# A gated linear attention and an MLP planned as one instruction list: first scores in other banks, denser filler products, finer pieces, a longer search for the order

## The chip, the cores and the metric

The kernel runs on one core of a Trainium2 chip. The metric is device time in microseconds (us) of one execution. The engines are named as in the profile: PE is TensorE (PEld its weight loads), DVE is VectorE, ACT is ScalarE, POOL is GpSimd, SP is the engine that issues most DMAs. "L795" is line 795 of the kernel before.

## What is computed

The first half is a gated linear recurrence over 768 steps for 4 x 8 heads of width 48; its output, rearranged to 3072 rows of 384, goes through a two-layer MLP with `h - tanh(h)` between the layers.

```python
for t in range(S):
    state = alpha[:, :, t, :, None] * state + np.einsum('bhd,bhe->bhde', k[:, :, t], v[:, :, t])
    y[:, :, t] = np.einsum('bhd,bhde->bhe', q[:, :, t], state)
...
x = np.ascontiguousarray(attn_out.transpose(0, 2, 1, 3)).reshape(B * S, H * D)
h = x @ w_in            # 384 -> 2048
g = h - np.tanh(h)
return (g @ w_out).astype(np.float32)
```

q, k, v and alpha are float32. The weights arrive as 8-byte words and are rounded to float32 on the chip.

## The kernel before

**Units.** The work is cut into 12 units of 256 time steps, all 8 heads of one batch entry each; a unit has two chunks of 128 steps, written `u.0` and `u.1`. For every unit there is an attention part (function `gla`) and an MLP part (`moe`) of 8 steps, written `u:0` to `u:7`.

**Attention part.** alpha, k and q come in by DMA. For unit 0, and for k and q of unit 1, they are turned by products with the identity (`turn`, L663; parts a and b are the even and the odd time steps) into PSUM. For all later ones ACT moves a strip of 16 columns (`widen`, two copies, L633) and DVE transposes 32x32 blocks (`flip`, four instructions, L639). Then DVE scans alpha from behind (`U`, L711), takes the ends (two small operations, L719 and L720) and scans from the front (`W`, L730); k is multiplied with U (`kU`) and q with W (`qW`) (L679 for the turned units). In unit 0 each scan is done in two halves, one for each chunk; in later units it is one instruction over both. After that, for each chunk: `scores` (PE, L795 or L805), `masked` (DVE, L819 or L822), `back`, `natural` and `update` (the state's increment), and `y` (PE, L850 to L860 in unit 0), then a copy into xT (`x`, ACT).

**MLP part.** Step `u:s` has `first` (PE, L1080, 12 products), four element-wise operations on ACT and DVE, and `second` (PE, L1125 in units 0 and 1, L1146 with the combined weights of `combine` after that). Weight pieces `in0` to `in7` and `out0` to `out7` are fetched by SP (L43), read by ACT (`read`, L86 and L87) and finished by DVE (L89 and L90), just ahead of unit 0's steps.

**PSUM.** [...] `ps_sc` holds one tile of two banks (`two_banks()`, name `sc`), `ps_h` two banks (tag `h`), `ps_o` four banks (tags `o0` to `o3`). In unit 0, alpha's turned parts lie in `o0` and `o1`, k's in the two `h` banks, and q's two parts in `sc`. `scores 0.0` then takes `sc` too, so it has to wait until every read of q's turned parts is over; `scores 0.1` takes the two `h` banks. Unit 1's turned q takes `sc` again.

**The order.** No engine's order is written by hand. Every piece of work is a task with an engine, an estimated duration, the tasks it depends on, and a latency to its dependents (0.3 us if nothing else is given). `Planner.run` (L341) is a list scheduler over these estimates; `Planner.order` (L387) calls it in 8 rounds, from the fourth with random noise (deviation 2 us) on the priorities, and keeps the plan that ends first. Two tasks of one engine that depend on each other are 0.3 us apart in it. All instructions are then issued in the order of the planned starts, and each engine works through its own list in that order.

**Filler.** Until the first `y` of unit 0, gaps in PE's plan are filled with products of the identity with itself (`spin`, L1208), whose result nobody reads. The number in each gap is the gap divided by an estimated 0.35 us, rounded down:

```python
filled += [(free, -1, do, None)] * int(max(0.0, x[0] - free) / us)
...
plan.filler = "PE", "y 0.0", 0.35, spin
plan.begin.update(SP=0.8, PE=1.5, ACT=3.0, DVE=4.8)
```

A float32 product leaves two matmul records in the profile.

Of the kernel before, what the change touches and what calls it, by code (L numbers as in the profile page):

```python
# [321 lines left out]
class Planner:  # L322
# [2 lines left out]

    ROUNDS, SEED, NOISE = 8, 1, 2.0

    def __init__(self):  # L330
        self.tasks = []
# [55 lines left out]
    def order(self):  # L387
        names = {t[0]: i for i, t in enumerate(self.tasks)}
        assert len(names) == len(self.tasks)
        before, after = ([[] for _ in self.tasks] for _ in range(2))  # L390
        for i, t in enumerate(self.tasks):
            edges = {names[a]: self.tasks[names[a]][6] for a in t[4]}
            if t[7]:
                edges.setdefault(names[t[7]], 0.0 if self.tasks[names[t[7]]][1] == t[1] else 0.25)
            for j, lat in edges.items():
                before[i].append((j, lat))
                after[j].append((i, lat))
        chance = random.Random(self.SEED)
        priority, late, best = [t[3] for t in self.tasks], None, None
        for n in range(self.ROUNDS):  # L400
            starts, order = self.run(priority, before, after, late if n % 2 else None, self.begin)
            ends = [s + t[2] for s, t in zip(starts, self.tasks)]
            if best is None or max(ends) <= best[0]:
                best = max(ends), starts, order
                turned, _ = self.run([-e for e in ends], after, before)
                back = [r + t[2] for r, t in zip(turned, self.tasks)]
                fair = [max(back) - b for b in back]
            late = fair if n < 4 else [x + chance.gauss(0, self.NOISE) for x in fair]
            priority = late
        _, starts, order = best  # L410
        plan = sorted(((starts[i], n, self.tasks[i][5], i) for n, i in enumerate(order)), key=lambda x: x[:2])

        engine, until, us, do = self.filler
        filled, free = [], self.begin.get(engine, 0.0)
        for x in plan:
            name, e, length = self.tasks[x[3]][:3]
            if e == engine and until:
                filled += [(free, -1, do, None)] * int(max(0.0, x[0] - free) / us)
                free = x[0] + length
                until = until if name != until else None  # L420
            filled.append(x)
        return filled


def fast(tc, q, k, v, alpha, moe_w_in, moe_w_out, out, w_in, w_out, ident, ok, pad_rows):
# [17 lines left out]
    with ExitStack() as ctx:  # L443
# [159 lines left out]
        def gla(u, rank):  # L603
# [5 lines left out]
            m = {}  # L609

            parted = u == 0
            parts = [(x, slice(c * NP, (c + 1) * NP), slice(c, c + 1)) for c, x in enumerate("ab")] if parted else [("", slice(0, N), slice(0, CU))]

            direct = u == 0

            def go(name, engine, us, k, after, do, of=u, **kw):
                add(f"{name} {of}", engine, us, rank + k,
                    [a if a[-1] in "0123456789" else f"{a} {of}" for a in after if a], do, **kw)

            prev = f" {u - 1}" if u > 0 else None  # L620
            for what, name in enumerate(("aT", "kT", "qT", "v")):
                go(f"load {name}", "SP", 1.3 if direct or what == 3 or by_matmul(u, what) else 2.2, -9 + 0.1 * what,
                   [what < 3 and u > 0 and not by_matmul(u - 1, what) and not by_matmul(u, what) and f"{name}{prev}"]
                   + [u == 1 and ("kUba 0" if what == 3 else "turn qTb 0")]
                   + [f"{last} {u - 2}.{CU - 1}" for last in ("y", "state") if what == 3 and u > 1
                      and (last == "y" or (u - 2) % UPB < UPB - 1)],
                   lambda what=what: load(u, what), lat=2.9 if u == 0 else 3.6 if u < PLAIN else 4.5)

            def widen(what):
                for hh in range(2):  # L630
                    t, r0 = raws[what], HP * hh
                    to, of = t[r0 + 32:r0 + HP, :, :, 0:D - 32], t[r0:r0 + 32, :, :, 32:D]
                    A.copy(to, of)  # L633

            def flip(what, make):
                t = make()
                for g in range(NP):
                    to = t[:, g].rearrange("p c (i r) -> p r c i", r=R)
                    V.transpose(to, raws[what][:, g, :, 0:32])  # L639

            def new(name):
                m[name] = two.tile([P, CU, NP, P], FP32, name=name)
# [39 lines left out]
            for n, ab in enumerate("ab"):  # L682
                if by_matmul(u, 0):
                    go(f"turn aT{ab}", "PE", 0.92, n * 0.1, ["load aT", later and "masked 0.0"], lambda n=n: turn(0, n))
                    go(f"aT{ab}", "DVE" if n else "ACT", 0.62, 0, [f"turn aT{ab}"], lambda n=n: place(n))
                if by_matmul(u, 1):
                    go(f"turn kT{ab}", "PE", 0.92, 1 + n * 0.1,
                       ["load kT"] + [later and x for x in ("x 0.0", "y 0.1", "state 0.1")], lambda n=n: turn(1, n))
                    for x, _, cs in parts:
                        go(f"kU{ab}{x}", "DVE", 0.33 if x else 0.6, 3, [f"turn kT{ab}", f"U{x}", n and f"kUa{x}", later and "back 0.1", later and by_matmul(u, 2) and "turn qTb"],  # L690
                           lambda n=n, cs=cs: times(1, "U", n, cs))
                if by_matmul(u, 2):
                    go(f"turn qT{ab}", "PE", 0.92, 2 + n * 0.1,
                       ["load qT", later and f"aT{ab}" if by_matmul(u, 0) else "masked 0.0"], lambda n=n: turn(2, n))
                    for x, _, cs in parts:
                        go(f"qW{ab}{x}", "DVE", 0.33 if x else 0.6, 5, [f"turn qT{ab}", f"W{x}", n and f"qWa{x}", later and "y 0.1", later and by_matmul(u, 1) and "turn kTb"],
                           lambda n=n, cs=cs: times(2, "W", n, cs))
# [55 lines left out]
            whole = [x for x, _, _ in parts]  # L753
            go("least", "DVE", 0.07, 7, [f"U{x}" for x in whole], shortest)
            if not by_matmul(u, 1):
                go("kU", "DVE", 1.12, 3, ["kT", "U"], lambda: scale("kT", "U"))
            if not by_matmul(u, 2):
                go("qW", "DVE", 1.12, 5, ["qT", "W"], lambda: scale("qT", "W"))
# [11 lines left out]
            def chunk(c):  # L770
# [43 lines left out]
                def masked():  # L814
                    sc = m["sc", c]
                    if direct:
                        m["pm", c] = [two.tile([P, NP, P], FP32, name=f"pm{r}", tag=tag) for r, tag in enumerate("zw")]
                        for r, to in enumerate(m["pm", c]):
                            V.tensor_mul(to, sc[r] if c else sc[:, r], mask.unsqueeze(1).to_broadcast([P, NP, P]))  # L819
# [144 lines left out]
                    go_c("scores", "PE", 1.27, 7, kU(u, c) + qW(u, c) + [f"natural {u}", f"load v {u}"] + held, scores)  # L964
                    go_c("masked", "DVE", 0.61, 8, ["scores", (u > 1 or c) and f"y {past}"], masked)
                if n > 0:
                    go_c("decay", "DVE", 0.27, 6, [f"ends{'ab'[c] if parted else ''} {u}", f"state {past}"], decay)
# [236 lines left out]
        def spin():  # L1204
# [1 line left out]
            if not spun:  # L1206
                spun.append(ps_o.tile([P, P], FP32, name="spin", tag="o2"))
            T.matmul(spun[0], lhsT=ident, rhs=ident, start=True, stop=True)  # L1208
# [113 lines left out]
```

## Time and profile before

| | us |
|---|---|
| three runs | 575.77, 576.29, 578.61 |
| median of them | 576.29 |
| the profiled execution, its own time | 578.48 |
| span of that execution | 576.7 |
| PE busy | 565.9 (98%) |
| DVE busy | 450.8 (78%) |
| ACT busy | 323.2 (56%) |
| mean granted clock of PE | 0.992 |

The profiled execution is one of the longer ones: 2.19 us above the median. The span leaves out 1.78 us around it. A share of busy time is an average: this kernel has a head of some 30 us, in which PE waits for the first unit, a middle in which PE is busy all the time, and an end of some 8 us. "PEclk" is the clock that PE was granted, in tenths or as a share of full speed.

### The profile page before, as it was taken

How to read it: one execution, taken by the hardware profiler on the slowest of the kernel's cores; microseconds unless marked ns; L12 is line 12 of the kernel's file. 1: busy time of each engine (PE TensorE's matmuls, PEld its weight loads, DVE VectorE, ACT ScalarE, POOL GpSimd, SP SyncE). 2: the span in 40 equal slices, each digit the busy share in tenths (PEclk: the TensorE clock that was granted, in tenths of full speed). 3: DMA queues.
4: the chain of work that ended last, by engine and by line, in shares of the span. 5: the costliest groups of instructions: out<-in, count | busy, mean ns of one | idle time of the engine just before them, and what ended most of it. 6: DMA issues, size and time to landing. Idle time of an engine off the chain costs nothing.

```text
span 576.7 us, 13746 instructions
## 1 busy us (share of the span) xinstructions
PE 565.9 (98%) x5583; PEld 500.1 (87%) x5583; DVE 450.8 (78%) x886; ACT 323.2 (56%) x559; POOL 4.8 (1%) x22
## 2 busy tenths in 40 slices
PE   8899999999999999999999999999999999999995
PEld 8787777778989999998999999898998999899995
DVE  5889879999999995895895896896797645554643
ACT  2589885747777686577485365364443433333530
POOL 3000000000000000000000000000000000000000
PEclk9799999999999999999999999999999999999999
DMA  8988781235674762562640320310200000000001
GB/s 181 211 220 243 233 182 56 85 70 137 113 155 120 121 161 84 118 158 71 185 116 1 85 61 3 75 51 22 53 12 1 30 7 3 28 8 0 28 1 35
DMA packets 60713, 50.84 MB, mean 88 GB/s; under 512 B 35776, under 2 KB 50400, under 8 KB 60640
## 3 DMA queue, kind: packets, MB, share of 16 engines
q1 hardware_dynamic: 57728, 48.88, 34.7%
q10 hardware_dynamic: 2912, 0.98, 0.8%
q8 instruction: 46, 0.75, 0.6%
q14 instruction: 27, 0.22, 0.1%
HBM read 44.04 MB, written 4.72 MB: 85 GB/s over the span
## 4 chain that ended last, share of the span: by engine, by line
PE 96%; DVE 2%; issue 1%; POOL 0%; ACT 0%; DVEq 0%; POOLq 0%
PE h L1080 43%; PE o L1146 32%; PE o L1125 7%; PE sc L805 2%; PE sc L878 2%; PE sc L888 2%; PE sc L811 2%; PE sc L991 1%; PE spin L1208 1%; PE turned L663 1%; DVE W L730 0%; PE sc L795 0%; PE h L795 0%; DVE w_in L90 0%; PE y L853 0%
## 5 line engine op out<-in xcount | busy, mean ns | idle before, releaser
L1080 PE MATMUL h<-xT,w_in 128*128 128x256 f32 x1152 | 265.1, 380 | 0.6 <-DVE w_in L90 0.6
L1080 PEld LDWEIGHTS h<-xT,w_in 128*128 128x128 f32 x1152 | 215.4, 190 | 28.0 <-DVE w_in L90 0.7
L1089 ACT ACTIVATE u<-h 128x512 f32<-128x512 f32 x96 | 57.0, 594 | 180.7 <-PE h L1080 180.2
L1097 DVE TENSOR_TENSOR w<-h,u 128x512 f32<-128x512 f32 x96 | 65.8, 686 | 79.1 <-ACT u L1089 78.7
L1146 PE MATMUL o<-b,e 128*128 128x192 f32 x480 | 90.9, 326 | 0.0
L1146 PE MATMUL o<-w_out,e 128*128 128x192 f32 x320 | 81.5, 337 | 0.0
L1146 PEld LDWEIGHTS o<-b,e 128*128 128x128 f32 x480 | 80.2, 190 | 0.0
L1101 DVE SCALAR_TENSOR_TENSOR g<-z,w 128x512 f32<-128x512 f32 x96 | 65.3, 682 | 4.1 <-PE o L1125 1.3
L1146 PE MATMUL o<-b,g 128*128 128x192 f32 x320 | 65.1, 326 | 0.0
L1093 ACT ACTIVATE z<-u 128x512 f32<-128x512 f32 x96 | 60.4, 629 | 2.6
L1146 PEld LDWEIGHTS o<-w_out,e 128*128 128x128 f32 x320 | 55.7, 189 | 4.4
L1146 PEld LDWEIGHTS o<-b,g 128*128 128x128 f32 x320 | 54.2, 190 | 0.0
L1107 ACT ACTIVATE big<-u 128x1024 f32<-128x1024 f32 x48 | 50.4, 1049 | 0.0
L1125 PE MATMUL o<-w_out,g 128*128 128x384 f32 x128 | 44.0, 488 | 0.0
L1125 PEld LDWEIGHTS o<-w_out,g 128*128 128x128 f32 x128 | 24.1, 190 | 13.7
L1113 DVE TENSOR_TENSOR e<-g 128x256 f32<-128x256 f32 x80 | 33.4, 418 | 1.8
L1114 DVE TENSOR_TENSOR e<-g 128x256 f32<-128x256 f32 x80 | 33.3, 416 | 0.0
L639 DVE STREAM_TRANSPOSE aT<-ar 128x256 f32<-128x256 f32 x44 | 28.4, 645 | 2.8 <-ACT ar L633 1.7
L730 DVE TENSOR_TENSOR_SCAN W<-aT,before 128x1032 f32<-128x1032 f32 (+1 forms) x13 | 27.7, 2132 | 0.0
L711 DVE TENSOR_TENSOR_SCAN U<-aT,after 128x1032 f32<-128x1032 f32 (+1 forms) x13 | 27.6, 2129 | 0.1
L1115 DVE TENSOR_TENSOR e<-g 128x128 f32<-128x128 f32 x80 | 22.6, 283 | 0.0
L639 DVE STREAM_TRANSPOSE qT<-qr 128x256 f32<-128x256 f32 x40 | 20.5, 629 | 0.0
(141 smaller groups left out, 560.3 us busy)
## 6 DMA issues: line engine op xcount, KB each, us to landing
raw<-in_moe_w_out_dram SPq DMA_DIRECT2D x16, 768.0 KB, 4.8
raw<-in_moe_w_in_dram SPq DMA_DIRECT2D x80, 96.0 KB, 4.0
raw<-in_moe_w_in_dram SPq DMA_DIRECT2D x16, 288.0 KB, 5.1
vt<-in_v_dram SPq DMA_DIRECT2D x23, 192.0 KB, 4.1
ar<-in_alpha_dram SPq DMA_DIRECT2D x44, 96.0 KB, 2.5
kr<-in_k_dram SPq DMA_DIRECT2D x40, 96.0 KB, 3.3
qr<-in_q_dram SPq DMA_DIRECT2D x40, 96.0 KB, 2.3
out_dram<-cross SPq DMA_DIRECT2D x19, 96.0 KB, 1.7
```

Of the source, the lines that this page charges most:

```text
L639: V.transpose(to, raws[what][:, g, :, 0:32])
L730: V.tensor_tensor_scan(out=m["W"][:, ns].rearrange("p n t -> p (n t)"), data0=aT[:, a:z], data1=before[:, a:z], initial=0.0, op0=ALU.mult, ...
L1080: T.matmul(h[:, a, :], lhsT=w_in[:, j, f * P:(f + 1) * P], rhs=xT[u][:, j, :], start=(j == 0), stop=(j == KT - 1))
L1089: A.activation(m["u", s], m["h", s], AF.Square, scale=W_SCALE ** -1.5)
L1093: A.activation(m["z", s], m["u", s], AF.Square, bias=QB, scale=QA * W_SCALE)
L1097: V.tensor_mul(m["w", s], m["h", s], m["u", s])
L1101: V.scalar_tensor_tensor(out=g.rearrange("p a c t -> p (a c t)"), in0=m["z", s], scalar=QK, in1=m["w", s], op0=ALU.add, op1=ALU.mult)
L1107: A.activation(big, m["us", s // 2].rearrange("p s t -> p (s t)"), AF.Relu, bias=-U_FAST, scale=W_SCALE, accum_out=over[:, n:n + 1])
L1113: V.tensor_add(e[:, 0:2, :], g[:, 0], g[:, 1])
L1114: V.tensor_sub(e[:, 2:4, :], g[:, :, 1, :], g[:, :, 0, :])
L1125: T.matmul(m["o"][c], lhsT=g[:, a, c, :], rhs=w_out[:, f, :], start=(f == 0), stop=(f == FT - 1))
L1146: T.matmul(o[n][:, i], lhsT=g_, rhs=w_, start=(s_ == 0 and (n, i) in ((0, 0), (1, 0), (2, 1), (3, 0))), stop=(s_ == FS - 1), skip_group_ch ...
```

## The change

- `scores 0.0` no longer takes `sc` but the two `ps_o` banks `o0` and `o1`, which held the turned alpha. Unit 1's `turn qT` then depends on unit 0's reads of q's turned parts, in place of unit 0's `masked 0.0`.
- A filler product is estimated at 0.24 us in place of 0.35, and the gap is lengthened by 0.5 us before it is divided, if it is over 0.2 us.
- The estimated latency of unit 0's loads goes from 2.9 to 3.3 us.
- Between two tasks of one engine (but SP) the planned latency is 0 in place of 0.3.
- The scans of all units are done in two halves. `widen` is planned as two tasks and `flip` as four, in place of one each; their instructions stay the same.
- After the 8 rounds, 1200 further plans are tried: in each, every task's priority is moved with a chance of 1% by a random amount (deviation 8 us). A plan is kept if it does not end later than the best so far.

```diff
     ROUNDS, SEED, NOISE = 8, 1, 2.0
+    CHANGES, SHARE, WIDE = 1200, 0.01, 8.0
...
-            edges = {names[a]: self.tasks[names[a]][6] for a in t[4]}
+            edges = {names[a]: 0.0 if self.tasks[names[a]][1] == t[1] != "SP" else self.tasks[names[a]][6] for a in t[4]}
...
+                kept, waits = priority, late if n % 2 else None
...
+        for n in range(self.CHANGES):
+            tried = [x + chance.gauss(0, self.WIDE) if chance.random() < self.SHARE else x for x in kept]
+            starts, order = self.run(tried, before, after, tried if n % 2 else waits, self.begin)
+            end = max(s + t[2] for s, t in zip(starts, self.tasks))
+            if end <= best[0]:
+                best, kept = (end, starts, order), tried
...
-                filled += [(free, -1, do, None)] * int(max(0.0, x[0] - free) / us)
+                filled += [(free, -1, do, None)] * (int((x[0] - free + 0.5) / us) if x[0] - free > 0.2 else 0)
...
-                   lambda what=what: load(u, what), lat=2.9 if u == 0 else 3.6 if u < PLAIN else 4.5)
+                   lambda what=what: load(u, what), lat=3.3 if u == 0 else 3.6 if u < PLAIN else 4.5)
...
-                       ["load qT", later and f"aT{ab}" if by_matmul(u, 0) else "masked 0.0"], lambda n=n: turn(2, n))
+                       ["load qT"] + [later and f"qW{x}{y} 0" for x in "ab" for y in "ab"], lambda n=n: turn(2, n))
...
-                go(f"wide {name}", "ACT", 1.3, k_ - 0.5, [f"load {name}"], lambda what=what: widen(what))
-                go(name, "DVE", 1.9, k_, [f"wide {name}"] + ([f"y {u - 2}.{CU - 1}"] if u > 1 else []),
-                   lambda what=what: flip(what, makes[what]))
+                pieces_of(f"wide {name}", "ACT", 1.3, k_ - 0.5, [f"load {name}"], [lambda what=what, hh=hh: widen(what, hh) for hh in range(2)])
+                pieces_of(name, "DVE", 1.9, k_, [f"wide {name}"] + ([f"y {u - 2}.{CU - 1}"] if u > 1 else []),
+                          [lambda what=what, g=g: flip(what, makes[what], g) for g in range(NP)])
...
-            for x, ns, _ in parts:
-                go(f"U{x}", "DVE", 1.13 if x else 2.2, 1, (["aTa", "aTb"] if by_matmul(u, 0) else ["aT"])
+            for x, ns in scans:
+                go(f"U{x}", "DVE", 1.13, 1, (["aTa", "aTb"] if by_matmul(u, 0) else ["aT"])
...
-                go(f"W{x}", "DVE", 1.13 if x else 2.2, 3, [f"ends{x}"] + (qW(u - 1) + [f"sizeW{prev}"] if prev else []),
+                go(f"W{x}", "DVE", 1.13, 3, [f"ends{x}"] + (qW(u - 1) + [f"sizeW{prev}"] if prev else []),
...
-                    if u == 0 and c == 1:
-                        sc = m["sc", c] = [ps_h.tile([P, 2, TU], FP32, name="h").rearrange(
-                            "p a t -> p (a t)").rearrange("p (g t) -> p g t", t=P) for _ in range(2)]
+                    if u == 0:
+
+                        sc = m["sc", c] = [(ps_h if c else ps_o).tile([P, NP, P], FP32, name="scores", tag="h" if c else f"o{r}")
+                                           for r in range(2)]
...
-        plan.filler = "PE", "y 0.0", 0.35, spin
+        plan.filler = "PE", "y 0.0", 0.24, spin
```

The new helper splits one task into several that follow each other:

```python
def pieces_of(name, engine, us, k, after, dos):
    for x, do in enumerate(dos):
        go(name + f"/{x}" * (x < len(dos) - 1), engine, us / len(dos), k, after if x == 0 else [f"{name}/{x - 1} {u}"], do)
```

More of the change, by code (lines that the diff above doesn't have):

```diff
@@ L611, in gla @@
             parted = u == 0
-            parts = [(x, slice(c * NP, (c + 1) * NP), slice(c, c + 1)) for c, x in enumerate("ab")] if parted else [("", slice(0, N), slice(0, CU))]
+            scans = [(x, slice(c * NP, (c + 1) * NP)) for c, x in enumerate("ab")]
+            parts = [(x, ns, slice(c, c + 1)) for c, (x, ns) in enumerate(scans)] if parted else [("", slice(0, N), slice(0, CU))]
             direct = u == 0
@@ L626, in gla, with widen, flip @@
                       and (last == "y" or (u - 2) % UPB < UPB - 1)],
-                   lambda what=what: load(u, what), lat=2.9 if u == 0 else 3.6 if u < PLAIN else 4.5)
[L629 to L639, printed above, removed]
+                   lambda what=what: load(u, what), lat=3.3 if u == 0 else 3.6 if u < PLAIN else 4.5)
+            def widen(what, hh):
+                t, r0 = raws[what], HP * hh
+                to, of = t[r0 + 32:r0 + HP, :, :, 0:D - 32], t[r0:r0 + 32, :, :, 32:D]
+                A.copy(to, of)
+            def flip(what, make, g):
+                if g == 0:
+                    m["to", what] = make()
+                V.transpose(m["to", what][:, g].rearrange("p c (i r) -> p r c i", r=R), raws[what][:, g, :, 0:32])
             def new(name):
@@ L689, in gla @@
                     for x, _, cs in parts:
-                        go(f"kU{ab}{x}", "DVE", 0.33 if x else 0.6, 3, [f"turn kT{ab}", f"U{x}", n and f"kUa{x}", later and "back 0.1", later and by_matmul(u, 2) and "turn qTb"],
+                        go(f"kU{ab}{x}", "DVE", 0.33 if x else 0.6, 3, [f"turn kT{ab}"] + [f"U{y}" for y in x or "ab"] + [n and f"kUa{x}", later and "back 0.1", later and by_matmul(u, 2) and "turn qTb"],
                            lambda n=n, cs=cs: times(1, "U", n, cs))
@@ L693, in gla @@
                     go(f"turn qT{ab}", "PE", 0.92, 2 + n * 0.1,
-                       ["load qT", later and f"aT{ab}" if by_matmul(u, 0) else "masked 0.0"], lambda n=n: turn(2, n))
+                       ["load qT"] + [later and f"qW{x}{y} 0" for x in "ab" for y in "ab"], lambda n=n: turn(2, n))
                     for x, _, cs in parts:
-                        go(f"qW{ab}{x}", "DVE", 0.33 if x else 0.6, 5, [f"turn qT{ab}", f"W{x}", n and f"qWa{x}", later and "y 0.1", later and by_matmul(u, 1) and "turn kTb"],
+                        go(f"qW{ab}{x}", "DVE", 0.33 if x else 0.6, 5, [f"turn qT{ab}"] + [f"W{y}" for y in x or "ab"] + [n and f"qWa{x}", later and "y 0.1", later and by_matmul(u, 1) and "turn kTb"],
                            lambda n=n, cs=cs: times(2, "W", n, cs))
@@ L746, in gla @@
             kU, qW = done("kU", 1), done("qW", 2)
-            for x, ns, _ in parts:
-                go(f"U{x}", "DVE", 1.13 if x else 2.2, 1, (["aTa", "aTb"] if by_matmul(u, 0) else ["aT"])
+            for x, ns in scans:
+                go(f"U{x}", "DVE", 1.13, 1, (["aTa", "aTb"] if by_matmul(u, 0) else ["aT"])
                    + (kU(u - 1) + [f"sizeU{prev}", f"least{prev}"] if prev else []), lambda ns=ns: scan_U(ns))
                 go(f"ends{x}", "DVE", 0.3, 3, [f"U{x}"], lambda ns=ns: ends(ns))
-                go(f"W{x}", "DVE", 1.13 if x else 2.2, 3, [f"ends{x}"] + (qW(u - 1) + [f"sizeW{prev}"] if prev else []),
+                go(f"W{x}", "DVE", 1.13, 3, [f"ends{x}"] + (qW(u - 1) + [f"sizeW{prev}"] if prev else []),
                    lambda ns=ns: scan_W(ns))
-            whole = [x for x, _, _ in parts]
+            whole = [x for x, _ in scans]
             go("least", "DVE", 0.07, 7, [f"U{x}" for x in whole], shortest)
             if not by_matmul(u, 1):
-                go("kU", "DVE", 1.12, 3, ["kT", "U"], lambda: scale("kT", "U"))
+                go("kU", "DVE", 1.12, 3, ["kT"] + [f"U{x}" for x in whole], lambda: scale("kT", "U"))
             if not by_matmul(u, 2):
-                go("qW", "DVE", 1.12, 5, ["qT", "W"], lambda: scale("qT", "W"))
+                go("qW", "DVE", 1.12, 5, ["qT"] + [f"W{x}" for x in whole], lambda: scale("qT", "W"))
             go("sizeU", "ACT", 1.08, 5, [f"U{x}" for x in whole], lambda: size("U", 0))
@@ L818, in masked @@
                         for r, to in enumerate(m["pm", c]):
-                            V.tensor_mul(to, sc[r] if c else sc[:, r], mask.unsqueeze(1).to_broadcast([P, NP, P]))
+                            V.tensor_mul(to, sc[r], mask.unsqueeze(1).to_broadcast([P, NP, P]))
                         return
@@ L966, in chunk @@
                 if n > 0:
-                    go_c("decay", "DVE", 0.27, 6, [f"ends{'ab'[c] if parted else ''} {u}", f"state {past}"], decay)
+                    go_c("decay", "DVE", 0.27, 6, [f"ends{'ab'[c]} {u}", f"state {past}"], decay)
                 if direct:
```

## The prediction

> **What bounds the kernel now.** I read the page first, then PE's waits, then the head (0 to 43 us) engine by engine in the timeline, then stretches by window. From the page:
>
> ```profile
> PE 565.9 (98%) x5583; PEld 500.1 (87%) x5583; DVE 450.8 (78%) x886; ACT 323.2 (56%) x559; POOL 4.8 (1%) x22
> PEclk9799999999999999999999999999999999999999
> PE 96%; DVE 2%; issue 1%; POOL 0%; ACT 0%; DVEq 0%; POOLq 0%
> ```
>
> PE is busy 98% of the span, but the row of its clock has one 7: in the second slice (14.4 to 28.8 us) the clock was not full. The whole list of PE's waits has three lines:
>
> ```profile
> PE sc L795 <- DVE qT L679: 2.0, 1, 2.0
> PE spin L1208 <- POOL ident masks.py:199: 1.6, 1, 1.6
> PE h L1080 <- DVE w_in L90: 0.6, 1, 0.6
> ```
>
> So after the head nothing can be gained by removing waits: from 31.07 us to the last product PE stops once, for 0.6 us at 42.25. Whatever the change gains lies in the head. PE there, from its timeline:
>
> ```profile
> 1.57 4.64 PE L1208 MATMUL spin<-ident 128*128 128x128 f32 x20 [1.57 <-POOL ident masks.py:199]
> 6.13 3.37 PE L663 MATMUL turned<-ident,rough 128*64 128x128 f32 x48
> ...
> 12.06 0.94 PE L1208 MATMUL spin<-ident 128*128 128x128 f32 x6
> 12.88 0.60 PE L925 MATMUL y<-ident,kT 112*128 112x112 f32 x4
> ...
> 14.70 0.94 PE L1208 MATMUL spin<-ident 128*128 128x128 f32 x6
> 17.64 2.08 PE L795 MATMUL sc<-qT,kT 48*128 48x128 f32 x16 [2.00 <-DVE qT L679]
> ```
>
> and the windows around it (columns: us, then busy time of the engines, PEclk, DMA share, GB/s):
>
> ```profile
> 17.64:19.65 2.01, 2.01 (x17) 1.79 (x17) 0.01 (x1) 0.00 (x0) 0.00 (x0) 0.50 0.78 183
> 19.65:23.60 3.95, 3.95 (x38) 3.37 (x36) 3.61 (x6) 2.82 (x5) 0.00 (x0) 0.50 1.20 255
> ```
>
> The reader is to see two losses. `scores 0.0` waits 2.0 us for DVE's last product with q's turned part (17.17 to 17.59 on DVE), though its own operands were ready at 15.99: that is the bank clash. After this thin stretch the clock is halved for about 6.7 us (17.6 to 24.3).
>
> DVE is the other half of the story. It is busy without a break from 8.76 to 17.6, waits 2.1 us for the scores, and is then full to 36 us:
>
> ```profile
> 8.76 0.69 DVE L670 COPY aT<-turned 128x512 f32<-128x512 f32 x1 [3.99 <-PE turned L663]
> 19.77 1.29 DVE L819 TENSOR_TENSOR pm<-sc,mask 128x512 f32<-128x512 f32 x2 [2.12 <-PE sc L795]
> 36.64 0.96 DVE L90 CUSTOM_DVE_ANT_0 w_in<-bits,more 128x1536 uint16<-128x1536 uint16 x1 [1.59 <-PE h L1080]
> ```
>
> So PE feeds DVE (alpha turned), DVE feeds PE (k, q, masks), and DVE with ACT makes the weight pieces for PE's first MLP steps.
>
> [...] the first turn (16 records) takes 1.7 us (6.13 to ACT's copy at 7.87), later ones 0.87, so the clock rose near 7.2; and it fell near 17.6 after 3.4 us in which PE did some 1.5 us of work (0.6 of `update`, 0.94 of filler). [...] an execution may escape the fall: I take that as the reason for 575.77 and 578.61 in the same three runs; no run here shows it directly. [...] a scan of 1032 takes 2.29, two of 516 start 1.13 apart.
>
> **The change part by part** (times on the profiled execution).
>
> First filler. Planned gap before: load 0.8 + 1.3 + 2.9 less PE's begin at 1.5 is 3.5, over 0.35 is 10 products, 20 records: as shown. After: 0.8 + 1.3 + 3.3 - 1.5 + 0.5 = 4.4, over 0.24 is 18 products, 36 records. At half clock a record takes 0.217 (20 from 1.57 to 5.91). Between 5.91 and 7.2 go 6 more; the other 10 at full clock, half of that each (a turn goes from 1.7 to 0.87 too), end at 8.3. alpha had landed by 4.6 (SP's fetch, waiting for it, goes on then), so these products only stand in its way. The first turn goes from 6.13 to 8.3; both parts of alpha are turned, at 0.87 each, by 10.1 in place of 8.75. **Cost +1.35** on DVE's start, and up to 1.8 if the clock rises earlier. Behind the filler in PE's queue stand all six turns.
>
> Later fillers. There are three gaps with 3 products each, so each was planned at 1.05 to 1.4 us; now 6 or 7 each, 18 to 21 products of 0.225 and some 0.1 to start each gap: 4.3 to 5.0 us of filler. The turns end at 13.5 (8.3 + 6 x 0.87), `back` and `update` take 1.02, so `scores 0.0` starts at 18.8 to 19.5. Its data are ready at 15.99 + 1.35 + 0.06 = 17.4 or, if the search orders DVE better, earlier. So **the bank edit is mostly eaten by the filler**: the wait of 2.0 goes, and filler late by 1.4 to 2.1 is next. From below, if the search closes the planned gaps, there is less filler and scores start at 17.4; from above 19.5. I take 18.8.
>
> Clock. With PE never idle the half-clock stretch goes. Scores take 1.05 in place of 2.08, the second ones too, and `y` 0.0 as well. Half of 6.7 is **3.35 of PE time, gain**; but DVE's two masks (1.22 each) then come to stand between scores and `y`. In order: scores to 19.85, mask to 21.1, second mask to 22.4 (24.0 if weight piece `in0` is put between, as before), `y 0.1` 2.85 long to 25.3 or 26.9, against 28.35. **Gain 1.4 to 3.0.**
>
> Turns of unit 1's q. Two of 0.9, until now behind `y`; freed from `masked 0.0` they can stand where filler stood, gain 0 to 1.8, if their load (issued at 18.93, landing 4.3 later) comes early enough. I take 0.4.
>
> What is late next: DVE. Its work up to piece `in3` (needed at 42.85) is unchanged but for the split: two halves and twice the ends in unit 1, 2 x 0.06 + 0.33 = 0.45. It starts 1.35 later, and loses its two idle times (2.12 and 1.59, less some 0.8 that stays): `in3` comes at 42.8 + 1.35 + 0.45 - 2.9 = 41.7. A better order (the second scan half or q's products of unit 1 after `in3`) can bring up to 2 more. I take 1.3: PE passes this point 2.4 earlier than before.
>
> Splits elsewhere: 10 units more x 0.45 on DVE lie beside PE, which is full; without that cover they cost 4.5. Transposes and copies only become separate tasks. Zero latency on one engine fits what the trace shows (dependent small operations follow within 0.2), and moves only the plan. The tail keeps its chain: last product, ACT, DVE, DMA.
>
> Sum: 576.7 - 2.4 = 574.3 span, and with 1.78 around it 576.1. Some of the three runs escape the halved clock anyway; the changed kernel should not meet it, so I put its median at **575.9**, 0.1% under the median of 576.29 and 0.45% under the profiled execution.
>
> **Rivals.**
> 1. *The filler gives back what the clock gains* (the forecast), 574.2 to 577.8, chance 0.48. For it: filler ahead of data that lie ready, and DVE full to 36 us.
> 2. *The head packs.* The search finds a plan without gaps before `y`, so that there is little filler; masks follow each other, weights come early, unit 1's turns hide: `y 0.1` ends at 24.5 (3.9 earlier) and 1.2 of turns are hidden: 571.6 + 1.8 = 573.4 or a little under; I say 573.2. For it: planned gaps of over a microsecond stood in the order. Against it: the 18 products at the front. Chance 0.17.
> 3. *Slower: order without slack in the full stretch.* The 1200 steps keep every plan that is not longer by the estimates, so tasks of DVE and ACT wander by many microseconds as long as PE has no planned gap. What real instructions need beyond the estimate then shows as stalls where there was one. Place: 90 to 565 us, where DVE is busy 42.2 of 43.5 us between 90 and 133.5, and 148.5 of 166.5 after. Price: each of 10 units has five attention groups on PE that wait for ACT and DVE; 0.15 us each is 7.5, with the gain of 2.4 taken off 581.2. It decides from 5.5 us of stalls after 43 us. Against it: the durations fit (a `cube` is 0.60 in plan and trace, a transpose 0.475), and PE itself is planned a little long. Chance 0.25.
> 4. *The edit does not do what it says*: the banks are free but PE comes at 19.5 with filler, the masks are split by `in0`, and DVE's late start goes through to `in3`: 578. Chance 0.10.
>
> **How the numbers follow.** This kernel's own runs differ by 0.5%, so 0.5% is what a measurement can tell from no change: 573.4 to 579.2. Faster: most of case 2 and the edge of 1, 0.17. Slower: nearly all of case 3 and the edge of 4, 0.25. Same: 0.58. The range for eight in ten goes from 573.0 (scores at 17.4 and the turns hidden) to 580.0 (case 3 with half its stalls); the forecast's own is 574.2 to 577.8.
>
> **What would show it.** Right: 36 records of filler before the first turn, which starts near 8.3; PEclk full after 8 us; no wait of `scores 0.0` for DVE, but filler right up to it; `y 0.1` done between 25 and 27; a DVE wait for `in3`, if any, before 41. Wrong: PE waits after 43 us of more than 2 in sum (case 3); far fewer filler records between the turns and `scores 0.0` (case 2); a half-clock stretch that stays; `turn aT` before 7 us.

## The result and the profile after

| | before | after |
|---|---|---|
| median of 4 runs, us | 576.37 | 591.94 (591.08 to 593.45) |
| ratio, 95% interval | | 1.0266 [1.0231, 1.0300] |
| profiled execution, span | 578.48, 576.7 | 591.08, 589.3 |

The change costs 15.6 us, where 575.9 was forecast and 580.0 was the upper end of the range. The page after, the rows of PE's busy time, its clock, and the shares of the chain that ended last:

```profile
PE 570.2 (97%) x5637; PEld 503.7 (85%) x5637; DVE 466.5 (79%) x930; ACT 324.8 (55%) x559; POOL 4.8 (1%) x22
PEclk9999999999999999999999999999999999999999
PE 57%; DVE 29%; issue 5%; DMA 4%; SPq 2%; ACT 1%; DVEq 0%; POOL 0%; ACTq 0%; POOLq 0%
```

The 7 in the clock's row is gone, as forecast. But the chain was PE for 96% and is PE for 57% now, with DVE at 29%: from a kernel in which PE sets the end it has become one in which PE waits for DVE many times. PE's longest waits after:

```profile
PE h L1094 <- DVE w L1111: 7.1, 7, 3.6
PE o L1160 <- DVE e L1127: 1.9, 3, 0.7
PE spin L1222 <- POOL ident masks.py:199: 1.6, 1, 1.6
PE sc L819 <- DVE xT L914: 0.8, 1, 0.8
```

The head, from PE's timeline:

```profile
1.57 6.41 PE L1222 MATMUL spin<-ident 128*128 128x128 f32 x36 [1.57 <-POOL ident masks.py:199]
7.91 2.84 PE L676 MATMUL turned<-ident,rough 128*64 128x128 f32 x48
...
18.79 1.52 PE L1222 MATMUL spin<-ident 128*128 128x128 f32 x12
20.24 2.06 PE L809 MATMUL scores<-qT,kT 48*128 48x128 f32 x32
...
42.17 2.83 PE L1094 MATMUL h<-xT,w_in 128*128 128x256 f32 x12 [3.64 <-DVE w L1111]
```

36 filler records, first turn at 7.91, and filler right up to the scores: the head is of the kind that was forecast, though the scores start at 20.24, where 19.5 was the latest. The single wait of 3.64 us at 42 and the many small ones after it were not in the forecast.

Where the time went is easiest to see in PE's waits of over 0.15 us, each put down to the moment when it ends; these are the stalls of the texts and tables below. In the kernel before there is one after 31 us, of 0.6 us. After the change they come to 3.6 us between 31 and 60 us and to 6.8 us in 12 places after 60 us, the last at 446. That is 10.5 us against 0.6, where the two spans differ by 12.6. The rest lies in shorter gaps and in the head.

### The profile page after: what moved, and what is told of

Its sections match the earlier page's. It is cut to its first block, busy times and chain, and to the rows that moved or that the text cites. A ratio compares the mean times of both kernels' runs of the same rounds, so it can differ in the third digit from the quotient of the medians.

```text
span 589.3 us, 13901 instructions
## 1 busy us (share of the span) xinstructions
PE 570.2 (97%) x5637; PEld 503.7 (85%) x5637; DVE 466.5 (79%) x930; ACT 324.8 (55%) x559; POOL 4.8 (1%) x22
## 4 chain that ended last, share of the span: by engine, by line
PE 57%; DVE 29%; issue 5%; DMA 4%; SPq 2%; ACT 1%; DVEq 0%; POOL 0%; ACTq 0%; POOLq 0%
PE h L1094 28%; PE o L1160 20%; DVE g L1115 3%; DVE w L1111 3%; DVE U L724 3%; DVE W L743 3%; DVE aT L652 2%; PE spin L1222 2%; DVE kT L652 2%; DVE qT L652 2%; DVE kT L748 2%; DMA raw<-in_moe_w_out_dram 1%; PE sc L892 1%; PE sc L819 1%; DMA ar<-in_alpha_dram 1%
## 5 line engine op out<-in xcount | busy, mean ns | idle before, releaser
L1160 PE MATMUL o<-w_out,e 128*128 128x192 f32 x320 | 79.7, 331 | 1.9 <-DVE e L1127 1.9
L1139 PEld LDWEIGHTS o<-w_out,g 128*128 128x128 f32 x128 | 24.1, 190 | 15.6 <-DVE g L1115 0.6
L743 DVE TENSOR_TENSOR_SCAN W<-aT,before 128x516 f32<-128x516 f32 x24 | 29.4, 1225 | 0.7
L724 DVE TENSOR_TENSOR_SCAN U<-aT,after 128x516 f32<-128x516 f32 x24 | 28.6, 1221 | 0.4
L914 DVE TENSOR_TENSOR xT<-sc,xT 48x256 f32<-48x256 f32 x40 | 16.7, 417 | 15.3 <-ACT xT L929 14.9
L929 ACT COPY xT<-sc 112x512 f32<-112x512 f32 x20 | 11.5, 576 | 21.7 <-PE sc L902 21.7
```

What stands on the lines that cost most here:

```text
L724: V.tensor_tensor_scan(out=m["U"][:, ns].rearrange("p n t -> p (n t)")[:, ::-1], data0=aT[:, z:a:-1], data1=after[:, a:z][:, ::-1], initia ...
L743: V.tensor_tensor_scan(out=m["W"][:, ns].rearrange("p n t -> p (n t)"), data0=aT[:, a:z], data1=before[:, a:z], initial=0.0, op0=ALU.mult, ...
L1139: T.matmul(m["o"][c], lhsT=g[:, a, c, :], rhs=w_out[:, f, :], start=(f == 0), stop=(f == FT - 1))
L1160: T.matmul(o[n][:, i], lhsT=g_, rhs=w_, start=(s_ == 0 and (n, i) in ((0, 0), (1, 0), (2, 1), (3, 0))), stop=(s_ == FS - 1), skip_group_ch ...
```

## Experiments

The theories at the start: the 1200 further plans use up slack (the prediction's third rival); the plan's estimates became too tight, by the zero latency or the finer pieces; the filler delays the head.

**Set 1: the search.** e1 is the change without the further plans, e2 the kernel before with them alone, e3 another seed, e4 300 plans in place of 1200.

The edits of e1 and e3 (e4 as e1, with 300; e2 adds the change's loop over the further plans and nothing else):

```diff
-    CHANGES, SHARE, WIDE = 1200, 0.01, 8.0
+    CHANGES, SHARE, WIDE = 0, 0.01, 8.0
```

```diff
-    ROUNDS, SEED, NOISE = 8, 1, 2.0
+    ROUNDS, SEED, NOISE = 8, 2, 2.0
```

> The changed kernel without the 1200 further plans; banks, filler, latencies and finer pieces stay. Wandering theory (the steps keep equally long plans and use up the slack): stalls of PE after 31 us fall from some 13 us to under 2, the 3.6 us wait near 38 us among them; time 575 to 578. Tight-estimate theory (zero latency on one engine and the finer pieces make PE wait): stalls of 8 us or more stay, time 585 to 592. Filler theory (the late start of the head causes the wait at 38 us): that wait of 3 to 4 us stays, the later ones go, 579 to 582.

> The kernel before, with the 1200 further plans and nothing else of the change. Wandering theory: PE stalls of 5 to 15 us in sum after 31 us, scattered over many places, time 582 to 592. Tight-estimate theory and filler theory: within 1.5 us of the kernel before, 575 to 578, since neither of their causes is in it.

> The changed kernel with another seed of the random numbers. Wandering theory: stalls of like sum (6 to 18 us) at other places, 583 to 595. Filler theory: the wait near 38 us is there again with 3 to 4 us. Tight-estimate theory: stalls at the same places as in the changed kernel.

> The changed kernel with 300 further plans in place of 1200. Wandering theory: fewer stalls than with 1200 but some, 2 to 8 us after 31 us, time 577 to 586. The other theories: as the changed kernel, 590 to 593.

| | median us | ratio to before, 95% | stalls 31-60, after 60 |
|---|---|---|---|
| e1 no search | 588.01 | 1.0189 [1.0154, 1.0225] | 3.2, 6.4 |
| e2 search alone | 577.26 | 1.0012 [0.9995, 1.0030] | 0, 0 |
| e3 other seed | 588.42 | 1.0194 [1.0161, 1.0228] | 1.0, 6.6 |
| e4 300 plans | 583.82 | 1.0126 [1.0089, 1.0164] | 3.7, 3.0 |

The wandering theory, my own favourite by then, falls from both sides as the cause: without the search the stalls stay, and the search alone makes none. e3 and e4 by themselves would have spoken for it: both lie in its ranges, while the tight-estimate theory had expected stalls at the places of the change (in e3 they are elsewhere) and 590 to 593 us (e4). The time does not follow the number of further plans, though (588.01 with none, 583.82 with 300, 591.94 with 1200), so what these two show is that one plan differs from the next by several us. The search found nothing by its own measure: of the 1200 plans 452 were kept, and none of them ended earlier by the planner's estimate than the plan it began with (569.83 us).

What DVE does in e1 points to the cause. Its timeline ahead of the longest wait, 4.49 us of PE for a new state:

```profile
168.99 0.68 DVE L1111 TENSOR_TENSOR w<-h,u 128x512 f32<-128x512 f32 x1
169.77 0.69 DVE L1115 SCALAR_TENSOR_TENSOR g<-z,w 128x512 f32<-128x512 f32 x1
170.50 0.42 DVE L1127 TENSOR_TENSOR e<-g 128x256 f32<-128x256 f32 x1
...
178.96 0.35 DVE L963 TENSOR_TENSOR state<-mid,sc 112x192 f32<-112x192 f32 x1
```

w, g and e depend on each other and stand in a row: w to g 0.78 us, g to e 0.73, where the plan counts 0.60 for each. The kernel before puts other work between them:

```profile
157.69 0.68 DVE L1097 TENSOR_TENSOR w<-h,u 128x512 f32<-128x512 f32 x1
158.29 2.67 DVE L639 STREAM_TRANSPOSE aT<-ar 128x256 f32<-128x256 f32 x4
160.80 0.68 DVE L1101 SCALAR_TENSOR_TENSOR g<-z,w 128x512 f32<-128x512 f32 x1
161.40 2.28 DVE L711 TENSOR_TENSOR_SCAN U<-aT,after 128x1032 f32<-128x1032 f32 x1
```

There w is followed after 0.60 and g after 0.60. Over the whole trace, g comes right behind a w 26 times of 96 before and 59 after; it is its own w in 25 and 48 of them (median 0.795 from start to start). e comes right behind its g 29 times of 80 before and 69 after (0.727). So the plan misses some 23 x 0.19 + 40 x 0.12 = 9.2 us more of DVE time than before, 6.5 of them between 60 and 300 us, where DVE has little to spare: before the change it is busy there for 215.67 of the 240 us, 90%.

```profile
60.00:300.00 240.00, 240.00 (x2315) 205.38 (x2314) 215.67 (x393) 166.90 (x297) 0.00 (x0) 1.00 0.53 127
```

(The columns are us, busy time of PE, PEld, DVE, ACT and POOL, clock, DMA share, GB/s.) These pairs are not the whole of it. Between 165 and 179 us of e1 they lose 0.5 us, and PE waits 4.49. The longest wait of the change itself, 3.64 us up to 42.17, has no such pair ahead of it on DVE:

```profile
38.66 0.96 DVE L90 CUSTOM_DVE_ANT_0 w_in<-bits,more 128x1536 uint16<-128x1536 uint16 x1 [2.37 <-PE h L1094]
...
40.21 1.23 DVE L743 TENSOR_TENSOR_SCAN W<-aT,before 128x516 f32<-128x516 f32 x1
41.36 1.26 DVE L1111 TENSOR_TENSOR w<-h,u 128x512 f32<-128x512 f32 x2
```

The first w could have run from 37.1, when ACT's u of that step was done. In DVE's list it stands behind a weight piece, for which DVE stood idle for 2.37 us until PE's product had ended, and behind half a scan. That is the order of the plan, and not lost time of a pair.

**Set 2: the latency and the pieces.** e5 is the whole change with 0.3 back, e6 the kernel before with the zero alone, e7 the change with whole scans and whole tasks, e8 the change with 0.17. The edit of e5; e6 is its reverse, e8 has 0.17 in place of the 0.0:

```diff
-            edges = {names[a]: 0.0 if self.tasks[names[a]][1] == t[1] != "SP" else self.tasks[names[a]][6] for a in t[4]}
+            edges = {names[a]: self.tasks[names[a]][6] for a in t[4]}
```

> The whole change, but the planned latency between two tasks of one engine back at 0.3. Latency theory (dependent DVE operations in a row take 0.12 to 0.19 us longer than planned, so zero latency lets DVE fall behind PE): stalls of PE after 31 us under 3 us, 575 to 579. Pieces theory (halved scans and pieces overfill DVE): stalls of 6 us or more stay, 583 to 590. Search theory is out as the only cause; if it adds its own, 579 to 583.

> The kernel before with zero latency on one engine and nothing else. Latency theory: stalls of 6 us or more after 31 us, 582 to 590, and two thirds or more of the cube-shrunk pairs directly behind each other on DVE. Pieces theory: as the kernel before, 575 to 578.

> The whole change, but scans of later units whole and the copies and transposes planned as one task each; zero latency and search stay. Latency theory: still 582 to 592, stalls of 6 us or more. Pieces theory: 575 to 579, stalls under 3 us.

> The whole change with 0.17 in place of 0 between two tasks of one engine, about what dependent DVE operations in a row lose in the traces (0.12 to 0.19). Latency theory: most of the stalls gone, 574 to 580. Pieces theory: 583 to 592.

| | median us | ratio to before, 95% | stalls 31-60, after 60 | g right behind w, of 96 |
|---|---|---|---|---|
| e5 latency back | 579.99 | 1.0060 [1.0043, 1.0077] | 2.4, 0.8 | 42 |
| e6 zero alone | 588.38 | 1.0208 [1.0169, 1.0247] | 3.2, 4.7 | 78 |
| e7 whole pieces | 585.01 | 1.0152 [1.0131, 1.0174] | 2.1, 5.1 | 57 |
| e8 0.17 | 585.24 | 1.0157 [1.0136, 1.0179] | 0.4, 2.9 | 46 |

The one line of e6 alone costs 12.2 us, where the whole change costs 15.6, and taking it back alone removes 12. e5 lies a little above the range of the latency theory, in that of a search that adds its own; e9 below tests that. e7 keeps its stalls without the pieces. e8 misses its range and lies in that of the pieces theory, which e7 rules out as the only cause. Its stalls did fall, from 10.5 us in the change to 3.3, but one of them is followed by 3.4 us at half clock, and 8.9 us lie behind PE's last product, where the other traces have 6.3 to 6.8. So e8 neither bears the lost time out nor refutes it.

In e6 the stalls after 31 us are 7.3 us above those of before, and the clock is halved for 13.7 us ahead of the end (17.4 to 27.6 and 222.2 to 225.6), where before has 6.8 (17.5 to 24.3). Half of the difference is 3.4 us, so stalls and clock together are 10.7 of the 11.1 us by which the spans differ. PE's waits in e6:

```profile
PE h L1080 <- DVE w L1097: 2.8, 2, 1.9
PE sc L795 <- DVE qT L679: 2.5, 1, 2.5
PE sc L805 <- ACT kn L996: 1.7, 1, 1.7
...
PE sc L878 <- DVE state L949: 1.2, 1, 1.2
```

**Set 3: which engine, and what is left.** e10 and e11 split the zero latency of e6 between DVE and the two others; e9 is e5 without the further plans.

```diff
-            edges = {names[a]: self.tasks[names[a]][6] for a in t[4]}
+            edges = {names[a]: 0.0 if self.tasks[names[a]][1] == t[1] == "DVE" else self.tasks[names[a]][6] for a in t[4]}
```

```diff
-            edges = {names[a]: self.tasks[names[a]][6] for a in t[4]}
+            edges = {names[a]: 0.0 if self.tasks[names[a]][1] == t[1] and t[1] in ("PE", "ACT") else self.tasks[names[a]][6] for a in t[4]}
```

> The kernel before with zero latency between two tasks of DVE only. DVE theory (dependent DVE operations in a row are what the plan misses): 582 to 590, stalls over 5 us after 31 us. Any-engine theory (any shift of the plan does it): the same as zero on PE and ACT, 578 to 586 for both.

> The kernel before with zero latency between two tasks of PE or two of ACT, DVE keeps 0.3. DVE theory: 575 to 579, stalls under 2 us. Any-engine theory: 578 to 586.

> The whole change with the latency between tasks of one engine back at 0.3 and without the 1200 further plans. If the search makes the 3.8 us that were left with the latency back: 575 to 577.5, stalls under 1.5. If the pieces or the filler make them: 578 to 581.

e10 took 586.26, 1.0160 [1.0119, 1.0201], with stalls of 4.7 and 1.9; e11 took 583.31, 1.0102 [1.0062, 1.0141], with 1.2 and 1.3. DVE is the larger part, but e11 is outside what the DVE theory allowed, and inside what the any-engine theory expected. ACT has dependent operations too: its second operation of a step comes 0.63 after the first when it stands right behind it, and something else came after 0.47 at best. It does so 76 times of 96 before, 89 in e11 and 72 in the change, so this can't be what the change lost. Some of e11's cost is clock: it is halved from 17.4 to 27.6, 10.2 us in place of 6.8, an estimated 1.7 us of PE's time. In all 16 runs of the four kernels that put zero latency into the kernel before (e6, e10, e11, e16) the mean granted clock is 0.983 to 0.990, and none of the 42 runs of before beside e10 and e11 is under 0.991 (beside e16 two of 42 are, with 0.987). e10 also limits what the pairs can explain: it has nearly as many as e6 (g right behind a w 65 times, e behind its g 72 times, against 78 and 79) and waits only 1.9 us after 60.

e9 took 579.23, 1.0039 [1.0025, 1.0052], with 0.4 and 0 us of stalls. The search thus costs nothing that shows with the latency back either, and what is left over the kernel before, some 3.3 us, is not stalls but lies in the head.

**Set 4: lost time or lost margin, and the head.** e16 is e6 with longer planned lengths (shrunk 0.79, sums 0.98, quad 0.66), which hold what dependent operations were seen to lose. e13 and e14 put the filler alone and the banks alone into the kernel before; in both, all other instructions keep the order of before. e15 is e9 with the filler and the load latency of before. One of the three length edits of e16, and the edit of e13 (the first gap is lengthened by 0.9, for the 18 products of the change):

```diff
-                add(f"shrunk {me}", "DVE", 0.6, r + 1,
+                add(f"shrunk {me}", "DVE", 0.79, r + 1,
```

```diff
-                filled += [(free, -1, do, None)] * int(max(0.0, x[0] - free) / us)
+                filled += [(free, -1, do, None)] * (int((x[0] - free + (0.5 if filled and free > 2.0 else 0.9)) / us) if x[0] - free > 0.2 else 0)
...
-        plan.filler = "PE", "y 0.0", 0.35, spin
+        plan.filler = "PE", "y 0.0", 0.24, spin
```

> The kernel before with zero latency on one engine, but with planned lengths that hold what dependent operations in a row were seen to lose (shrunk 0.79, sums 0.98 on DVE, quad 0.66 on ACT). Lost-time theory (the plan stalls because it misses this time): stalls under 3 us after 31 us, 575 to 580. Margin theory (0.3 was more than the loss, and the surplus is what kept PE fed): still 581 to 588.

> The kernel before with the changed filler alone: 18 products ahead of the first turn and 6 in each later gap, the order of all else that of before, to the instruction. Filler theory (what is left with the latency back is the head's late start): first turn near 8.3, scores 0.0 not before 18.5, 577 to 580. If the fuller clock pays for it: 575 to 577.

> The kernel before with the bank edit alone, the order of all instructions that of before. Scores 0.0 start at 16.0 to 16.4 in place of 17.6; the half-clock stretch goes or comes later. If the wait was on the path: 574 to 575.7. If DVE's weight pieces bind: 575.7 to 576.5.

> The whole change with 0.3 between tasks of one engine, no further plans, and the filler and load latency of before; banks and finer pieces stay. Filler theory: the 3.3 us that were left go, 574.5 to 577. If the finer pieces cost them: 578 to 580.

| | median us | ratio to before, 95% | first turn | scores 0.0 | first 0:3 | stalls 31-60, after 60 |
|---|---|---|---|---|---|---|
| e16 | 586.56 | 1.0172 [1.0146, 1.0198] | 6.13 | 18.20 | 48.55 | 3.5, 1.4 |
| e13 filler alone | 577.57 | 1.0018 [1.0006, 1.0031] | 8.10 | 19.07 | 42.35 | 0.6, 0 |
| e14 banks alone | 576.53 | 0.9992 [0.9975, 1.0008] | 5.38 | 14.76 | 38.35 | 1.4, 1.2 |
| e15 | 576.27 | 0.9999 [0.9984, 1.0015] | 5.71 | 14.06 | 38.19 | 0.4, 0 |

e16 answers by stretch. From 60 us on the stalls fall from 4.7 (e6) to 1.4, although g stands right behind a w 74 times: with the missed time planned, most of them go. But the longer lengths are planned for every such operation, also where nothing is lost, so they give margin too, and this run does not part the two. The windows of 60 to 300 us say the same, first e6, then e16:

```profile
60.00:300.00 240.00, 235.27 (x2329) 200.56 (x2329) 216.38 (x383) 164.05 (x287) 0.00 (x0) 0.99 0.52 128
```

```profile
60.00:300.00 240.00, 238.64 (x2356) 203.39 (x2355) 220.68 (x392) 169.19 (x295) 0.00 (x0) 1.00 0.52 131
```

Between 31 and 60 us e16 still stalls for 3.5 us, and its clock is halved from 17.8 to 28.1 and from 48.6 to 52.0; `first 0:3` starts 5.7 us later than before (48.55 against 42.85), and so the time stays. The unit-1 operations there (scans, ends, products) kept their old lengths. Whether longer lengths for these would mend the head too was not tried. So the choice between lost time and lost margin stays open, for the head above all.

e13 is the filler's price by itself: 1.0 us [0.3, 1.8]. e15 against e9, 576.27 against 579.23, shows that in the changed plan filler and load latency cost more, 3.0. With this the whole is taken apart step by step: the change 591.94, with the latency back 579.99 (e5), without the further plans 579.23 (e9), with the old filler and load latency 576.27 (e15), beside 576.12 for the kernel before. e14 is the bank edit's worth by itself: nothing that shows in the time. Its PE timeline shows why:

```profile
14.76 1.16 PE L795 MATMUL scores<-qT,kT 48*128 48x128 f32 x16 [0.41 <-DVE qT L679]
...
25.78 0.87 PE L663 MATMUL sc<-ident,rough 128*64 128x128 f32 x10 [0.70 <-DMA rough<-in_q_dram]
26.58 5.45 PE L1080 MATMUL h<-xT,w_in 128*128 128x256 f32 x24
```

The scores come 2.9 us earlier than in the profile before and the first MLP step 4.5 earlier. The edit's own part of the 2.9 is some 1.6, the wait for DVE that falls from 2.00 to 0.41; the rest is that the same 20 filler records and the turns ran faster in this execution (first turn at 5.38 in place of 6.13). Then PE waits for what comes next, four times between 55 and 96 us, 2.2 us in all. The waits of the whole trace for weight pieces are:

```profile
PE h L1080 <- DVE w_in L90: 1.4, 3, 0.7
PE o L1125 <- DVE w_out L90: 0.7, 1, 0.7
```

Three of the four, and three quarters of the time, are waits for weight pieces. The head's gain is given back there. The profile names DVE, which finishes a piece, but DVE itself was waiting. First ACT, then DVE:

```profile
45.13 1.08 ACT L86 ACTIVATE more<-raw 128x768 int16<-128x768 uint32 x1 [1.58 <-DMA raw<-in_moe_w_out_dram]
```

```profile
47.16 0.96 DVE L90 CUSTOM_DVE_ANT_0 w_out<-bits,more 128x1536 uint16<-128x1536 uint16 x1 [1.53 <-ACT more L87]
...
55.09 0.96 DVE L90 CUSTOM_DVE_ANT_0 w_out<-bits,more 128x1536 uint16<-128x1536 uint16 x1 [1.51 <-ACT more L87]
```

The `w_out` pieces landed at 45.04, 53.00 and 58.13, and ACT read them from 45.13, 53.08 and 58.21. Followed back, these waits begin at transfers that landed late, and not at a DVE that was full. What the transfers cost is not shown, since no run here changed them.

**Set 5: versions that keep a part.** e12 is e14 with 7 filler products ahead of the first turn (0.5 us each in the division, since a product took 0.43 us there in the profile before, 20 records in 4.34) and 0.24 in the later gaps, nothing added. e17 is the same filler in e15.

The edit of e17 (e12 tells the first gap by another test, with the same count):

```diff
-                filled += [(free, -1, do, None)] * int(max(0.0, x[0] - free) / us)
+                filled += [(free, -1, do, None)] * int(max(0.0, x[0] - free) / (us if free > 2.0 else 0.5))
...
-        plan.filler = "PE", "y 0.0", 0.35, spin
+        plan.filler = "PE", "y 0.0", 0.24, spin
```

> The kernel before with the bank edit, 7 filler products ahead of the first turn in place of 10, 4 in place of 3 in each of the three later gaps (estimate 0.24, nothing added to the gap); the order of all else is that of before, to the instruction. If the head is bound as I read it: first turn at 4.8 to 5.2, scores 0.0 at 15.5 to 16.5, no half-clock stretch, 573.0 to 575.3, so 1 to 3 us under before. If DVE's weight pieces bind instead: 575.3 to 576.5, no change.

> The bank edit and the finer pieces with 0.3 between tasks of one engine, no further plans, 7 filler products ahead of the first turn and gaps divided by 0.24 with nothing added. If the start of DVE's chain still counts: first turn near 4.9, 573.5 to 575.5, below the kernel before. If the weight pieces bind: 575.5 to 576.5.

e12 took 575.26, 0.9970 [0.9957, 0.9984]; e17 575.41, 0.9977 [0.9964, 0.9989]. The first turn starts at 4.85 and 4.68, as expected. By their medians both are 0.7 to 0.8 us under the kernel before; the ratios, in which the longer runs of before count too, say 1.7 and 1.3. That is the one part of the change's idea that pays, and little, because `w_in` binds next (a wait of 1.1 us up to 64.17 in e12, 1.8 us of waits in e17).

## Why the prediction was wrong

**The step that failed** is in the change part by part: "Zero latency on one engine fits what the trace shows (dependent small operations follow within 0.2), and moves only the plan." I had the number in hand and priced it at nothing. Within 0.2 is not zero: 0.12 to 0.19 us for each dependent pair, on an engine that is 90% busy from 60 to 300 us. And moving "only the plan" is moving everything, since the plan is the order of all engines. Alone it costs 12.2 us (e6), and taking it out of the change removes 12.0 (e5). The 0.3 of before did two things: it left room for this loss, and it made the scheduler put independent work between dependent operations (26 pairs w-g side by side before, 78 in e6). That these two are how the zero does its harm is my reading; how much each carries is not shown, and the wait up to 42.17 in the change shows that the order makes stalls without such a pair.

**A second term was mis-sized**, and would have made the forecast wrong without the first. The head was to gain 2.4 us net. With the latency back and no further plans the time is 579.23 (e9), 3.3 above the kernel before, and the filler with the load latency is 3.0 of it (e15).

**The third rival** had the place right (stalls in the full stretch, DVE behind, from 5.5 us of stalls on; 6.8 were measured after 60) and the cause wrong: the 1200 plans make no stall by themselves (e2) and their absence removes few (e1). That its place came true is luck. Its sum has a slip: 581.2 is 576.1 + 7.5 - 2.4, and 576.1 has the gain of 2.4 in it already, so the price gives 583.6. Half of it was too low an upper end for the range.

**The head** was right in kind, and too early for the scores and `y`. First turn forecast 8.3, measured 7.91. Scores forecast at 18.8, at most 19.5, measured 20.24: there were four gaps ahead of them, with 23 products, in place of three with 18 to 21. `y 0.1` forecast done by 25.3 to 26.9, measured 28.7, a further gap with 5 products standing ahead of `y 0.0`. The clock stayed full: 1.00 in every window up to 49 us. That filler eats the bank edit holds: with the banks alone (e14) the scores start at 14.76, with both (e9) at 19.25, filler right up to them.

**The weight pieces as the next bound** hold: e14, e12 and e17 run into them. That DVE's work is what makes them late does not: where PE waited for them in e14, DVE was waiting for ACT and ACT for the transfers. **Splits elsewhere** beside PE at no cost holds too: e15 has them all and is at 0.9999.

**The clock** as the reason for the spread of before is borne out for most of it. The 42 runs beside e12 lie in two groups, 25 of them at 575.50 to 576.15 and 17 at 576.83 to 579.24. Each run's mean granted clock is known: it is 0.994 or more in all of the first group. In 12 of the second it is 0.991 or 0.992, as in the traced execution with its half-clock stretch (0.992); in the other five it is 0.996 to 0.998, and their time has another reason. With the bank edit no run shows it: 0.996 or more in all 14 of e14 and all 22 of e12. That the half-clock stretch goes when PE is never idle was the author's estimate, from one fall in one trace: PE was busy for 1.44 of the 3.44 us from 14.20 to 17.64, and the clock reads 0.50 from there to 24.3. What sets off the fall is not shown. Nor is a low clock in the first 7 us, which the forecast inferred from the length of the products there (0.43 us each): the profile's clock reads 1.00 from 1.57 to 7.20.

What stays open beside the head: kernels with zero latency on all three engines range from 583.8 to 591.9 with plans that differ by a seed or a step count. Differences among them (e7 against the change, e1 against e4) may be the plan's accident, so I give no part of the 15.6 us to the pieces or the search on their account. The two groups do not overlap, though: all seven plans with zero latency (the change, e1, e3, e4, e6, e7, e16) take 583.8 us or more, and those with 0.3 (before, e2, e5, e9, e15) 580.0 or less. Zero latency is the one large effect that is shown on both sides, by adding it and by taking it away. By what path it costs the time is shown in part only.

## What to carry to other kernels

In a list scheduler for engines that work in order, a latency between dependent operations of one engine need not be waste: here it left room for the 0.12 to 0.19 us that such a pair lost, and it made the scheduler put other work between them. Before an estimate is cut, count how often the trace has the pair right behind each other and what it loses there, and multiply by the count that the new order would have. The product says what the plan misses, not what the new order will cost. An engine named as the cause of a wait can itself be waiting (DVE for 1.53 us in e14): follow its own wait one step back before calling it the bound. Filler put in for the sake of the clock (0.996 or more in all 21 runs of e13) should end before the data it waits for; ahead of the first real work, where a product took 0.43 us (before) against 0.24 in a later gap (e9), that takes fewer, not more.

## What the runs showed of the hardware that was not expected

A stall in the full stretch cost twice in two runs. In e1 PE waited for 4.49 us up to 179.46, and the clock was at half for 6.8 us from 177.2; in e8, with a wait of 2.4 us at 177, it was at half for 3.4 us from 179.8; the windows, first of e1, then of e8:

```profile
171.00:177.20 6.20, 3.97 (x77) 3.22 (x76) 6.04 (x12) 6.05 (x12) 0.00 (x0) 1.00 0.53 122
177.20:184.00 6.80, 4.54 (x72) 4.45 (x73) 6.52 (x17) 4.50 (x9) 0.00 (x0) 0.50 0.34 65
```

```profile
174.00:179.80 5.80, 3.35 (x78) 3.01 (x77) 5.70 (x12) 4.62 (x9) 0.00 (x0) 1.00 0.03 6
179.80:183.20 3.40, 3.40 (x12) 3.40 (x12) 3.39 (x7) 3.29 (x7) 0.00 (x0) 0.51 0.57 167
```

In e8 PE was busy for the whole 3.4 us at 0.51 of its clock, so an estimated 1.7 us were lost on top of the wait. Ahead of the end, the half-clock stretches of these traces last 3.4 us (e6, e8, e16), 6.8 (before, e1, e10) or 10.2 (e6, e11, e16). PE was not idle in the 3.4 us ahead of them: it was busy for 0.96 us in e8 and for 1.75 in e6, where the wait had been 1.7 us long:

```profile
218.74:222.15 3.41, 1.75 (x68) 1.42 (x67) 3.27 (x7) 3.31 (x6) 0.00 (x0) 1.00 0.41 115
```

The 3.6 us wait of the changed kernel, at 38.5 to 42.2, was followed by no such stretch (the clock reads 1.00 from 38.5 to 49.0); the length of the wait alone did not decide.
